# Where the weights' sums of a seven-product block are made, and 96 bytes less of padding

## Chip, cores, metric

One core of a Trainium2 chip runs the whole kernel as one program. The metric is the device time of one execution in microseconds (us). Of the kernel before, three executions were timed (median 883.89 us, 883.29 to 884.83), and one more was recorded by the profiler.

## What is computed

A linear attention feeds a two-layer feed-forward block, all in float32:

```python
q_s = softmax(q, axis=-1)            # 8 batches, 8 heads, 576 positions, 64 wide
k_s = softmax(k, axis=2)             # over the positions
kv  = einsum('bhsd,bhse->bhde', k_s, v)
x   = einsum('bhsd,bhde->bhse', q_s, kv)   # to 4608 tokens x 512
out = (maximum(x @ w_in, 0) ** 2) @ w_out  # 512 -> 2048 -> 512
```

## The kernel before

**Tiles.** The 4608 tokens are worked in nine tiles of 512: tile t (0 to 7) has the first 512 positions of batch t, and tile 8 the last 64 positions of all eight batches. The 2048 inner columns are 16 chunks f of 128. For each chunk TensorE (PE) makes `h` (128 x 512, line 100's helper, `first`) from w_in's chunk and x, VectorE (DVE) and ScalarE (ACT) square its positive part, and PE adds its product with w_out's chunk to four accumulators `acc` (`second`), two chunks behind `first`. Every float32 factor is split into a high and a low part (`gh`, `gl`, `xh`, `xl`, and two halves of each weight), and each product is three matmuls of 512 columns: high by high, high by low, low by high. So a chunk's `h` is 12 matmuls and its `acc` another 12. `h` has two PSUM buffers: `h` of chunk f + 2 can begin only when DVE has written `gl` of chunk f, which reads `h` last.

**Beside that.** While tile t runs, DVE, ACT, GpSimd (POOL) and the DMA queue of SyncE (SP) prepare the attention of batch t + 1, one pair of heads after another. Near a tile's beginning (f = 1) and at f = 5, 9 and 13, DVE runs a chain of small operations on `bst` (the row statistics of q, 128 x 18), a product with q and a transpose; it begins when a swap of `bst` between partitions by four small DMAs has landed. POOL takes the column maximum of k over the partitions (`kmx`). Each engine runs its instructions in order; the order of tile 0 is made by a planner, everything behind it runs in the order of the code.

**The joint block.** Tiles 7 and 8 are worked together, two chunks at a time (eight pairs n), by seven products in place of eight half-size ones: with a11 to a22 the quarters of the pair's weights (rows are the pair's two chunks, columns the two halves of the inner dimension) and b11 to b22 those of the tokens, the products need the weights' sums s1 = a21 + a22, s2 = s1 - a11, s3 = a11 - a21, s4 = a12 - s2, and the tokens' differences t1 to t4 (`ahead`, in tile 6). A product is six matmuls of 512 columns, in the order a11, a12, s2, s1, s3, a22, s4. Two PSUM buffers A and Bk take them; DVE and ACT combine them to c11, c22, c21 and c12. Of these, c11 and c21 (tile 7) are split to gh and gl at once (`use_g`), and c22 and c12 (tile 8) are stored to memory (`keep_g`, `g_last`). Between the products, units of three matmuls of the pair before (`unit`) are worked off.

**The sums before.** In tiles 1 to 4, at f = 1 and 9, `full_sums` and `add_sums` make one pair's sums on POOL (two additions of 512 columns, four operations of 256). At f = 3 and 11 `begin_sums` stores the pair's a11, a12 and a22 to the memory tensor `w_sums` of that pair, at f = 4 and 12 the sums are split (ACT casts, DVE subtracts), and at f = 7 and 15 `keep_sums` stores them. The joint block loads all seven pieces of a pair one or two pairs ahead (`load_weights`), into slabs 0, 1, 14 and 15 for even pairs and into other buffers (`ring`) for odd ones. A slab is one chunk of w_in, high and low part. Slabs 4 to 13 hold the tokens' pieces there; t3's low part lies in slab 13.

**Memory.** In SBUF the pools stand one behind the other: const, att, cvt, ffn, tiny, and then `boot`, which is closed after the start and replaced by `late`. Weights are held as 16 words of two chunks each (word 0 has chunks 0 and 1 of w_in, word u from 1 to 14 has chunk u + 1 of w_in and u - 1 of w_out, word 15 the last two of w_out); words 0 to 11 lie in const and 12 to 15 in `late`. `tiny`, the small pool, begins with a pad of 92 numbers (line 398), `late` with one of 16.

Of the kernel before, what the change touches and what calls it, by code (L numbers as in the profile page):

```python
# [10 lines left out]
F32 = mybir.dt.float32  # L11
F32R = mybir.dt.float32r
# [4 lines left out]
ALU = mybir.AluOpType  # L17
# [319 lines left out]
def attention_ffn(  # L337
# [29 lines left out]
    P = 128  # L367
# [27 lines left out]

    const, att, cvt = pool("const", 1), pool("att", 1), pool("cvt", 2)
    ffn, tiny = pool("ffn", 2), pool("tiny", 1)
    tiny.pool.tile([P, 92], F32, tag="pad2", name="pad2")
    boot_ctx = ExitStack()
    boot = Pool(boot_ctx.enter_context(tc.tile_pool(name="boot", bufs=3)), 3, True)  # L400
    ps_o, ps_h, ps_a = (pool(n, d, space=PSUM) for n, d in (("ps_o", 1), ("ps_h", 2), ("ps_a", 1)))
# [637 lines left out]
    def second(f, parts, acc, c, begin=0, end=NF - 1):  # L1039
        gh, gl = parts  # L1040
        cs = slice(c * P, (c + 1) * P)
        with plan.together(True):
            for n, (a, w) in enumerate(((gh, wo_h), (gh, wo_l), (gl, wo_h))):
# [2 lines left out]
                    start=(f == begin and n == 0), stop=(f == end and n == 2),  # L1046
                )

    def begin_sums(j):

        one, two = slabs[2 * j], slabs[2 * j + 1]
        for q, (slab, cols) in enumerate(
            ((one, slice(0, HM)), (one, slice(HM, M)), (two, slice(HM, M)))
        ):
            Y.dma_start(
                out=w_sums[j][:, 4 * q + 2:4 * q + 4, :], in_=slab[:, :, cols].bitcast(F32)
            )

    def full_sums(j):

        one, two = slabs[2 * j], slabs[2 * j + 1]
        full = cvt.tile([P, 2, M], F32, tag="w", name=f"full_{j}")
        for i, slab in enumerate((one, two)):
            G.tensor_tensor(out=full[:, i, :], in0=slab[:, 0, :], in1=slab[:, 1, :], op=ALU.add)
        made["full", j] = full

    def add_sums(j):

        full = made.pop(("full", j))
        (a11, a12), (a21, a22) = ((full[:, i, 0:HM], full[:, i, HM:M]) for i in range(2))  # L1070
        sums = cvt.tile([P, 4, HM], F32, tag="w", name=f"sums_{j}")
        s1, s2, s3, s4 = (sums[:, n, :] for n in range(4))
        G.tensor_tensor(out=s1, in0=a21, in1=a22, op=ALU.add)
        G.tensor_tensor(out=s2, in0=s1, in1=a11, op=ALU.subtract)
        G.tensor_tensor(out=s3, in0=a11, in1=a21, op=ALU.subtract)
        G.tensor_tensor(out=s4, in0=a12, in1=s2, op=ALU.subtract)
        made["sums", j] = sums.rearrange("p n c -> p (n c)")

    def split_sums(j):

        sums = made.pop(("sums", j))
        hi = cvt.tile([P, 2, M], F32R, tag="w", name=f"sums_h_{j}").rearrange("p t n -> p (t n)")
        lo = sums.bitcast(F32R)
        for i in range(2):
            S.copy(out=hi[:, i * M:(i + 1) * M], in_=sums[:, i * M:(i + 1) * M])
        made["split", j] = hi, lo, sums

    def rest_sums(j):

        hi, lo, sums = made["split", j]  # L1090
        for i in range(2):
            at = slice(i * M, (i + 1) * M)
            V.tensor_tensor(out=lo[:, at], in0=sums[:, at], in1=hi[:, at], op=ALU.subtract)
# [29 lines left out]
        return w  # L1123

    SOURCE = {"s1": 0, "a11": 2, "s2": 4, "a12": 6, "s3": 8, "a22": 10, "s4": 12}

    def load_weights(n, w, *names):

        for name in names if w else ():
            at = SOURCE[name]  # L1130
            Y.dma_start(out=w[name].bitcast(F32), in_=w_sums[n][:, at:at + 2, :])

    def pieces(name, t):

# [241 lines left out]
    def sums_step(t, f):  # L1376

        j, i = divmod(f, NF // 2)
        j += 2 * (t - 1)
        if t < 1 or j >= NF // 2:  # L1380
            return
        if i == 1:
            full_sums(j)
            add_sums(j)
        elif i == 3:
            begin_sums(j)
        elif i == 4:
            split_sums(j)
            rest_sums(j)
        elif i == 7:  # L1390
            keep_sums(j)

    x_of, w_of = {}, {}
# [1 line left out]
    def take(name, eng, out, in0, in1):  # L1395

        for i in range(2):
            eng.tensor_tensor(out=out[i], in0=in0[i], in1=in1[i], op=ALU.subtract)
        made[name] = out
# [7 lines left out]
    def ahead(f, x):  # L1407

        k = range(2)
        if f == 4:  # L1410
            made["b11"] = [x[:, i, :] for i in k]
            made["b21"] = [x[:, 2 + i, :] for i in k]
            made["b12"], made["b22"] = (
                [slabs[X_RAW + j].bitcast(F32)[:, i, :] for i in k] for j in range(2)
            )
            for i in k:
                to = slabs[X_RAW + i].bitcast(F32)[:, :, 0:(B - 1) * TL]
                Y.dma_start(out=to, in_=x_tail[:, 2 * i:2 * i + 2, 0:(B - 1) * TL])
            w_of[0] = weights(0)
            load_weights(0, w_of[0], "a11", "s1", "a12", "s2")  # L1420
        elif f == 6:
            split_x_of("b11")
        elif f == 9:
            temps = [att.tile([P, M], F32, tag=tag, name=f"sum_{tag}") for tag in ("k", "q")]
            take("t1", G, temps, made["b12"], made["b11"])
        elif f == 11:
            split_x_of("t1")
        elif f == 12:
            split_x_of("b21")
            take("t2", V, made["t1"], made["b22"], made["t1"])  # L1430
        elif f == 13:
            split_x_of("t2")
            take("t3", V, made["b11"], made["t2"], made["b11"])
        elif f == 14:
            split_x_of("t3")
            take("t4", V, made["b21"], made["b21"], made["t2"])
        elif f == 15:
            load_weights(0, w_of[0], "s3", "a22", "s4")
            split_x_of("b22")
# [63 lines left out]
    def unit(count):  # L1503

        for t, f, parts_u, acc_u, c, begin, end in units[:count]:
            second(f, parts_u, acc_u, c, begin=begin, end=end)
            if f == end:
                store(t, acc_u, c)
        del units[:count]
# [6 lines left out]
    def use_g(f, c, tags, eng):  # L1516

        V.scalar_tensor_tensor(out=c, in0=c, scalar=0.0, in1=c, op0=ALU.max, op1=ALU.mult)
        split_last(f, c, tags, eng, WT)
# [21 lines left out]
    for n in range(PAIRS):  # L1541
        one, two = 2 * n, 2 * n + 1
        units_at = (0, 1, 1, 1, 1) if n else (3, 0, 1, 0, 0)
        w = w_of.pop(n)
        A, Bk = (ps_h.tile([P, M], F32, tag="h", name=f"h_{WT}_{f}") for f in (two, one))
        u1, u2, u3 = (
            ffn.tile([P, M], F32, tag=tag, name=f"u_{tag}_{n}", bufs=1) for tag in ("xh2", "xl2", "xh3")
        )
        c11, c21 = (ffn.tile([P, M], F32, tag="r", name=f"c_{WT}_{f}") for f in (one, two))
        c22, c12 = (att.tile([P, M], F32, tag="ek", name=f"c_{B}_{f}", bufs=2) for f in (two, one))  # L1550
        if n == 0:
            split_x_of("t4")
        unit(units_at[0])

        product(A, w["a11"], x_of["b11"], True)
        S.copy(out=u1, in_=A)
        unit(units_at[1])
        product(Bk, w["a12"], x_of["b21"], True)
        V.tensor_tensor(out=c11, in0=Bk, in1=u1, op=ALU.add)
        use_g(one, c11, one_tags, G)  # L1560
        if n == PAIRS - 1:
            load_g(0)
            load_g(1)
        unit(units_at[2])
        product(A, w["s2"], x_of["t2"], False)
        S.copy(out=u2, in_=A)
        if n == 0:
            w_of[1] = weights(1)
            load_weights(1, w_of[1], "a11", "s1", "a12", "s2", "s3", "a22", "s4")
        elif n + 2 < PAIRS:  # L1570
            w_of[n + 2] = weights(n + 2)
        unit(units_at[3])
        product(Bk, w["s1"], x_of["t1"], True)
        if n == 0:
            w_of[2] = weights(2)
        load_weights(n + 2, w_of.get(n + 2), "a12", "s2", "a11", "s1")
        unit(units_at[4])
        product(A, w["s3"], x_of["t3"], False)
        S.copy(out=u3, in_=A)
        V.tensor_tensor(out=c22, in0=Bk, in1=u3, op=ALU.add)  # L1580
        keep_g(two, c22)
        if n == PAIRS - 1:
            load_g(2)
        unit(2)
        product(A, w["a22"], x_of["t4"], False)
        load_weights(n + 2, w_of.get(n + 2), "s3", "a22")
        S.copy(out=c21, in_=A)
        unit(1)
        product(Bk, w["s4"], x_of["b22"], False)
        load_weights(n + 2, w_of.get(n + 2), "s4")  # L1590
        V.tensor_tensor(out=c12, in0=Bk, in1=u2, op=ALU.add)
        tags = ((att, "v", 2), (att, "k" if n % 2 else "q", None))
        use_g(two, c21, tags, V)
        keep_g(one, c12)
        if n == PAIRS - 1:
            load_g(3)
        unit(1)
        if acc is None:
            acc = begin_acc(WT)
        units += [(WT, f, parts[WT, f], acc, c, 0, NF - 1) for f in (one, two) for c in range(C)]  # L1600
# [54 lines left out]
```

## Time and profile before

| | |
|---|---|
| median of three timed executions | 883.89 us |
| the profiled execution | 886.97 us |
| its span, first to last instruction | 885.2 us |
| instructions | 12559 |
| data moved | 95.52 MB |
| q1, the queue of SP and ACT: share of 16 DMA engines | 36.2% |

The profile names an instruction by its line, engine, operation and tiles, written left of the arrow and read right of it; nearly all instructions are recorded through one helper at line 100, so one goes by the tiles' names. A timeline row has start, duration, engine and shape, and in brackets how long the engine stood idle before and what ended that. A row of the chain that ended last has start, duration and what ran. In group rows the numbers behind the bar are busy time in us and the mean of one in ns. PE's rows of duration 0.39 overlap, since matmuls are pipelined; the pace is the distance between starts. Places in the span: tile 0 begins about 61 us in, tile 2 at 234, tile 5 at 524, and the joint block at 711.

### The profile page before, as it was taken

To read this page: it belongs to the slowest core of one execution; us is meant where nothing else is said; L and a number is where in the kernel's file an instruction comes from. 1 tells how busy PE (TensorE), PEld (TensorE's weight loads), DVE (VectorE), ACT (ScalarE), POOL (GpSimd) and SP (SyncE) were. 2 spreads that over 40 slices of the span, in tenths; PEclk is the share of its full clock that TensorE was granted. 3 is DMA by queue.
4 is the path that set the end of the run, shared out by engine and by line. 5 is a ranking of instruction groups with operands and counts; after the bars stand their busy time and mean duration, and the time that the engine had idled before them with its cause. 6 is when DMAs were issued, how large, how long until landed. Compare 5 with 4: busy or idle time off the path is not lost.

```text
span 885.2 us, 12559 instructions
## 1 busy us (share of the span) xinstructions
PE 862.2 (97%) x4408; PEld 705.4 (80%) x4408; DVE 571.2 (65%) x1092; ACT 377.5 (43%) x719; POOL 181.2 (20%) x211
## 2 busy tenths in 40 slices
PE   7899999999999999999999999999999999999997
PEld 6678877788878887888878888888887888888786
DVE  6988978766676767666766766676677653433421
ACT  5888854333533343334433353334343432222221
POOL 6789982020020202020202000000001001010000
PEclk9999999999999999999999999999999999999999
DMA  9992121413433243323232242122341175542432
GB/s 283 387 325 58 36 50 66 110 51 84 130 86 86 70 131 85 87 74 92 73 87 74 74 139 51 27 50 63 87 120 34 36 238 156 170 149 81 153 115 48
DMA packets 164367, 95.52 MB, mean 108 GB/s; under 512 B 113104, under 2 KB 146384, under 8 KB 164304
## 3 DMA queue, kind: packets, MB, share of 16 engines
q1 hardware_dynamic: 162592, 93.41, 36.2%
q10 hardware_dynamic: 1712, 1.31, 0.5%
q8 instruction: 35, 0.57, 0.3%
q14 instruction: 28, 0.23, 0.1%
HBM read 64.88 MB, written 29.23 MB: 106 GB/s over the span
## 4 chain that ended last, share of the span: by engine, by line
PE 81%; DVE 7%; DMA 4%; SPq 3%; ACT 2%; issue 1%; DVEq 0%; ACTq 0%
PE acc L100 40%; PE h L100 28%; PE h L1157 9%; SPq L100 3%; DVE bst L100 3%; PE x L100 3%; PE kv L100 2%; DMA raw<-in_moe_w_out_dram 2%; DMA k<-in_k_dram 1%; DVE q L100 1%; DMA bst<-bst 1%; DVE km L100 1%; DVE gl L100 1%; DVE h L100 1%; DVE qT L100 0%
## 5 line engine op out<-in xcount | busy, mean ns | idle before, releaser
L100 PE MATMUL acc<-w,gh 128*128 128x512 f32 x1152 | 357.9, 392 | 0.0
L100 PE MATMUL h<-xh,w 128*128 128x512 f32 x896 | 298.7, 396 | 8.3 <-DVE v L100 6.0
L100 PEld LDWEIGHTS acc<-w,gh 128*128 128x128 f32 x1152 | 214.8, 188 | 46.1 <-ACT gh L100 0.4
L100 PE MATMUL acc<-w,gl 128*128 128x512 f32 x576 | 225.5, 392 | 0.0
L100 PEld LDWEIGHTS h<-xh,w 128*128 128x128 f32 x896 | 169.1, 189 | 47.3 <-DVE v L100 7.7
L100 PE MATMUL h<-xl,w 128*128 128x512 f32 x448 | 176.0, 393 | 0.0
L100 PEld LDWEIGHTS acc<-w,gl 128*128 128x128 f32 x576 | 108.2, 188 | 24.2 <-DVE gl L100 0.4
L100 DVE TENSOR_TENSOR gl<-h,gh 128x512 fp32r<-128x512 f32 x112 | 77.2, 690 | 68.6 <-ACT gh L100 58.8
L100 ACT ACTIVATE gh<-r 128x512 fp32r<-128x512 f32 x112 | 70.7, 631 | 91.0 <-PE acc L100 89.3
L100 POOL PARTITION_ALL_REDUCE kmx<-km x24 | 17.1, 713 | 418.9 <-DVE km L100 418.9
L100 DVE SCALAR_TENSOR_TENSOR h<-h,r 128x512 f32<-128x512 f32 x112 | 77.2, 690 | 39.6 <-ACT r L100 39.0
L100 PEld LDWEIGHTS h<-xl,w 128*128 128x128 f32 x448 | 84.5, 189 | 17.1
L100 ACT ACTIVATE r<-h 128x512 f32<-128x512 f32 x112 | 66.4, 593 | 61.9 <-PE h L100 61.6
L100 ACT ACTIVATE q<-q 128x576 f32<-128x576 f32 (+1 forms) x32 | 21.5, 673 | 72.0 <-DVE q L100 70.8
L100 DVE TENSOR_REDUCE bst<-q 128x18 f32<-128x576 f32 x48 | 35.9, 748 | 13.9 <-ACT q L100 13.5
L100 DVE TENSOR_TENSOR bst<-bst 128x18 f32<-128x18 f32 (+1 forms) x96 | 29.0, 302 | 23.7 <-DMA bst<-bst 14.8
L100 POOL TENSOR_TENSOR w<-w,raw 128x512 int32<-128x512 int32 x32 | 42.1, 1323 | 7.7 <-DVE w L100 3.7
L100 DVE TENSOR_TENSOR c<-h,u_xh 128x512 f32<-128x512 f32 x16 | 11.1, 692 | 49.4 <-ACT u_xh L100 41.5
L100 POOL TENSOR_TENSOR w<-w,w 128x512 fp32r<-128x512 f32 x32 | 41.1, 1299 | 4.3 <-ACT w L100 4.2
L100 DVE TENSOR_TENSOR q<-q,bst 128x576 f32<-128x576 f32 x48 | 40.3, 839 | 1.7
L100 POOL TENSOR_TENSOR gl<-c,gh 128x512 fp32r<-128x512 f32 x8 | 10.3, 1292 | 131.0 <-ACT gh L100 131.0
L100 ACT ACTIVATE raw<-raw 128x1024 f32<-128x1024 f32 (+1 forms) x32 | 36.3, 1150 | 1.4 <-DMA raw<-in_moe_w_in_dram 1.1
(151 smaller groups left out, 960.5 us busy)
## 6 DMA issues: line engine op xcount, KB each, us to landing
k<-in_k_dram SPq DMA_DIRECT2D x32, 256.0 KB, 2.9
raw<-in_moe_w_in_dram SPq DMA_DIRECT2D x16, 512.0 KB, 8.6
raw<-in_moe_w_out_dram SPq DMA_DIRECT2D x16, 512.0 KB, 9.1
out_dram<-o SPq DMA_DIRECT2D x32, 256.0 KB, 2.4
v<-in_v_dram SPq DMA_DIRECT2D x56, 128.0 KB, 2.9
w<-w_sums SPq DMA_DIRECT2D x28, 256.0 KB, 3.3
q<-in_q_dram SPq DMA_DIRECT2D x96, 72.0 KB, 2.3
w_sums<-w SPq DMA_DIRECT2D x24, 256.0 KB, 3.1
```

Source lines behind the costliest of these rows:

```text
L100: getattr(self.eng, op)(*map(real, args), **{k: real(a) for k, a in kwargs.items()})
L1157: nc.tensor.matmul(out=out.real(), lhsT=a[:, k * P:(k + 1) * P].real(), rhs=m[k].real(), start=(begin and k == 0 and i == 0), stop=(k == 1 ...
```

## The change

Four things are edited.

- **Six pairs' sums move into the joint block.** `OWN = 2`: for pairs 2 to 7 the sums are made while the pair before is worked, by a new function `own_sums` in six steps placed between the products, and never stored. For these, `begin_sums` stores a21 as a fourth piece, `load_weights` skips s1 to s4, and `own_sums` loads a21 at the pair's beginning. Each step is two operations of 256 columns on DVE (eight additions and subtractions that also add the halves of a quarter, then four that take the high part off, behind four casts on ACT).
- **Two pairs' sums stay in the tiles**, pair 0 in tile 2 and pair 1 in tile 3, on DVE in place of POOL and spread over f = 4, 8, 10 and 12, with the split at f = 12 and 13 and the store at f = 14.
- **POOL's other subtractions on this path move to DVE**: t1 in tile 6 (from f = 9 to f = 10) and gl of c11 in every pair.
- **The pad** of the small pool has 68 numbers in place of 92: all of that pool behind the pad, and `boot` and `late`, move down by 96 bytes.

```diff
-    tiny.pool.tile([P, 92], F32, tag="pad2", name="pad2")
+    tiny.pool.tile([P, 68], F32, tag="pad2", name="pad2")
...
+    OWN = 2
...
+        for at, slab, cols in (
+            (2, one, slice(0, HM)), (6, one, slice(HM, M)), (10, two, slice(HM, M)),
+            (14, two, slice(0, HM)),
+        )[:3 if j < OWN else 4]:
+            Y.dma_start(out=w_sums[j][:, at:at + 2, :], in_=slab[:, :, cols].bitcast(F32))
...
-            G.tensor_tensor(out=full[:, i, :], in0=slab[:, 0, :], in1=slab[:, 1, :], op=ALU.add)
...
+        V.tensor_tensor(
+            out=made["full", j][:, i, :], in0=slab[:, 0, :], in1=slab[:, 1, :], op=ALU.add
+        )
...
+            if n >= OWN and name in SUMS:
+                continue
...
+    def own_sums(n, w, step):
...
+        if step == 0:
+            made["own"] = [
+                cvt.tile([P, 4, HM], F32, tag="w", name=f"own_{kind}_{n}") for kind in ("a", "s")
+            ]
+            Y.dma_start(out=made["own"][0][:, 0:2, :], in_=w_sums[n][:, 14:16, :])
+            return
...
+        for out, (in0, in1), op in (
+            ((a21, (a21, a22), ALU.add), (a22, two("a22"), ALU.add)),
+            ((a11, two("a11"), ALU.add), (a12, two("a12"), ALU.add)),
+            ((s1, (a21, a22), ALU.add), (s2, (s1, a11), ALU.subtract)),
+            ((s3, (a11, a21), ALU.subtract), (s4, (a12, s2), ALU.subtract)),
+            (), (),
+        )[step - 1]:
+            V.tensor_tensor(out=out, in0=in0, in1=in1, op=op)
+        if step > 4:
+            for i in (0, 1) if step == 5 else (2, 3):
+                hi, lo = two(SUMS[i])
+                S.copy(out=hi, in_=s[:, i, :])
+                V.tensor_tensor(out=lo, in0=s[:, i, :], in1=hi, op=ALU.subtract)
...
-            take("t1", G, temps, made["b12"], made["b11"])
+            take("t1", V, temps, made["b12"], made["b11"])
...
-        use_g(one, c11, one_tags, G)
+        use_g(one, c11, one_tags, V)
+        own_sums(n + 1, w_next, 1)
```

The instruction order of POOL behind tile 0: first the one before, from the third maximum of tile 1's batch to the second of tile 2's (`full` and `sums` are the sums, the bare ISA rows reload POOL's function library).

```order
L100 ISA kmx_3_2325<-km_3_2322 128x128
L100 ISA kmx_0_2618<-km_0_2615 128x128
L100 ISA
L100 TENSOR_TENSOR full_2672<-w_797 128x512
L100 TENSOR_TENSOR full_2672<-w_854 128x512
L100 TENSOR_TENSOR sums_2675<-full_2672 128x256
L100 TENSOR_TENSOR sums_2675<-sums_2675,full_2672 128x256
L100 TENSOR_TENSOR sums_2675<-full_2672 128x256
L100 TENSOR_TENSOR sums_2675<-full_2672,sums_2675 128x256
L100 ISA
L100 ISA kmx_1_2781<-km_1_2778 128x128
```

The same stretch of POOL now:

```order
L100 ISA kmx_2_2127<-km_2_2124 128x128
L100 ISA kmx_3_2302<-km_3_2299 128x128
L100 ISA kmx_0_2588<-km_0_2585 128x128
L100 ISA kmx_1_2744<-km_1_2741 128x128
L100 ISA kmx_2_2978<-km_2_2975 128x128
```

From tile 1 on POOL has nothing left but the maxima, and no reloads between them.

DVE in pair 2 of the joint block before, from c11 to the relu of c12 (`c_4` is first c11 and then c12, `c_5` first c22 and then c21):

```order
L100 TENSOR_TENSOR c_4_7175<-h_4_7168,u_xh_2_7163 128x512
L100 SCALAR_TENSOR_TENSOR c_4_7175<-c_4_7175 128x512
L100 TENSOR_TENSOR c_5_7217<-h_4_7168,u_xh_2_7215 128x512
L100 SCALAR_TENSOR_TENSOR c_5_7217<-c_5_7217 128x512
L100 TENSOR_TENSOR c_4_7247<-h_4_7168,u_xl_2_7191 128x512
L100 SCALAR_TENSOR_TENSOR c_5_7235<-c_5_7235 128x512
L100 TENSOR_TENSOR gl_5_7252<-c_5_7235,gh_5_7250 128x512
L100 SCALAR_TENSOR_TENSOR c_4_7247<-c_4_7247 128x512
```

And now, from the relu of c11 on (`own_a` holds a21, a22, a11, a12, `own_s` s1 to s4, `ring` the next pair's weights):

```order
L100 SCALAR_TENSOR_TENSOR c_4_7102<-c_4_7102 128x512
L100 TENSOR_TENSOR gl_4_7107<-c_4_7102,gh_4_7105 128x512
L100 TENSOR_TENSOR own_a_7081<-own_a_7081 128x256
L100 TENSOR_TENSOR own_a_7081<-ring_a_3_7048 128x256
L100 TENSOR_TENSOR own_a_7081<-ring_7012 128x256 x2
L100 TENSOR_TENSOR own_s_7135<-own_a_7081 128x256
L100 TENSOR_TENSOR own_s_7135<-own_s_7135,own_a_7081 128x256
L100 TENSOR_TENSOR c_5_7149<-h_4_7095,u_xh_2_7147 128x512
L100 SCALAR_TENSOR_TENSOR c_5_7149<-c_5_7149 128x512
L100 TENSOR_TENSOR own_s_7135<-own_a_7081 128x256
L100 TENSOR_TENSOR own_s_7135<-own_a_7081,own_s_7135 128x256
L100 TENSOR_TENSOR ring_7012<-own_s_7135,ring_7012 128x256 x2
```

Six sums and gl stand between c11 and c22; s3, s4 and the first two low parts stand between c22 and c12, the other two low parts behind c12's relu.

SP at the same place before, from the store of c12 of pair 1 to that of pair 2:

```order
L100 DMA g_last<-c_2_7144 128x512
L100 DMA w_382<-w_sums_111 128x512 x4
L100 DMA g_last<-c_5_7217 128x512
L100 DMA w_1487<-w_sums_111 128x512 x2
L100 DMA w_1576<-w_sums_111 128x512
L100 DMA g_last<-c_4_7247 128x512
```

And now:

```order
L100 DMA g_last<-c_2_7065 128x512
L100 DMA own_a_7081<-w_sums_110 128x512
L100 DMA w_382<-w_sums_111 128x512 x2
L100 DMA g_last<-c_5_7149 128x512
L100 DMA w_1487<-w_sums_111 128x512
L100 DMA g_last<-c_4_7183 128x512
```

Three loads of a pair's weights are left of seven, and the load of a21 stands right behind the store of the pair before.

More of the change, by code (lines that the diff above doesn't have):

```diff
@@ L1047, in second @@
                 )
+    OWN = 2
     def begin_sums(j):
         one, two = slabs[2 * j], slabs[2 * j + 1]
[L1052 to L1063, printed above, removed]
-            G.tensor_tensor(out=full[:, i, :], in0=slab[:, 0, :], in1=slab[:, 1, :], op=ALU.add)
-        made["full", j] = full
@@ L1067, in add_sums @@
-    def add_sums(j):
-        full = made.pop(("full", j))
-        (a11, a12), (a21, a22) = ((full[:, i, 0:HM], full[:, i, HM:M]) for i in range(2))
[L1071 to L1077, printed above, removed]
+        for at, slab, cols in (
[3 more added lines that the diff above has]
+            Y.dma_start(out=w_sums[j][:, at:at + 2, :], in_=slab[:, :, cols].bitcast(F32))
@@ new lines, in full_sums, with add_sums @@
+    def full_sums(j, i):
+        if i == 0:
+            made["full", j] = cvt.tile([P, 2, M], F32, tag="w", name=f"full_{j}")
+        slab = slabs[2 * j + i]
+        V.tensor_tensor(
+            out=made["full", j][:, i, :], in0=slab[:, 0, :], in1=slab[:, 1, :], op=ALU.add
+        )
+    def add_sums(j, n):
+        full = made["full", j]
+        (a11, a12), (a21, a22) = ((full[:, i, 0:HM], full[:, i, HM:M]) for i in range(2))
+        if n == 0:
+            made["sums", j] = cvt.tile([P, 4, HM], F32, tag="w", name=f"sums_{j}")
+        s1, s2, s3, s4 = (made["sums", j][:, i, :] for i in range(4))
+        out, in0, in1, op = (
+            (s1, a21, a22, ALU.add), (s2, s1, a11, ALU.subtract),
+            (s3, a11, a21, ALU.subtract), (s4, a12, s2, ALU.subtract),
+        )[n]
+        V.tensor_tensor(out=out, in0=in0, in1=in1, op=op)
@@ L1079, in split_sums @@
     def split_sums(j):
-        sums = made.pop(("sums", j))
+        sums = made.pop(("sums", j)).rearrange("p n c -> p (n c)")
         hi = cvt.tile([P, 2, M], F32R, tag="w", name=f"sums_h_{j}").rearrange("p t n -> p (t n)")
-        lo = sums.bitcast(F32R)
         for i in range(2):
             S.copy(out=hi[:, i * M:(i + 1) * M], in_=sums[:, i * M:(i + 1) * M])
-        made["split", j] = hi, lo, sums
+        made["split", j] = hi, sums.bitcast(F32R), sums
     def rest_sums(j):
@@ L1125, in attention_ffn, with two @@
     SOURCE = {"s1": 0, "a11": 2, "s2": 4, "a12": 6, "s3": 8, "a22": 10, "s4": 12}
+    SUMS = "s1", "s2", "s3", "s4"
     def load_weights(n, w, *names):
         for name in names if w else ():
+            if n >= OWN and name in SUMS:
+                continue
             at = SOURCE[name]
             Y.dma_start(out=w[name].bitcast(F32), in_=w_sums[n][:, at:at + 2, :])
+    def own_sums(n, w, step):
+        if n < OWN or n >= PAIRS:
+            return
[4 more added lines that the diff above has]
+            Y.dma_start(out=made["own"][0][:, 0:2, :], in_=w_sums[n][:, 14:16, :])
+            return
+        a, s = made["own"]
+        a21, a22, a11, a12 = (a[:, i, :] for i in range(4))
+        s1, s2, s3, s4 = (s[:, i, :] for i in range(4))
+        def two(name):
+            return w[name][:, 0, :], w[name][:, 1, :]
+        for out, (in0, in1), op in (
[5 more added lines that the diff above has]
+        )[step - 1]:
+            V.tensor_tensor(out=out, in0=in0, in1=in1, op=op)
+        if step > 4:
[3 more added lines that the diff above has]
+                V.tensor_tensor(out=lo, in0=s[:, i, :], in1=hi, op=ALU.subtract)
     def pieces(name, t):
@@ L1379, in sums_step @@
         j += 2 * (t - 1)
-        if t < 1 or j >= NF // 2:
+        if t >= 1 and j < NF // 2 and i == 3:
+            begin_sums(j)
+        j = t - 2
+        if j not in range(OWN):
             return
[L1382 to L1387, printed above, removed]
+        if f == 4:
+            full_sums(j, 0)
+        elif f == 8:
+            full_sums(j, 1)
+        elif f == 10:
+            for n in range(3):
+                add_sums(j, n)
+        elif f == 12:
+            add_sums(j, 3)
             split_sums(j)
+        elif f == 13:
             rest_sums(j)
-        elif i == 7:
+        elif f == 14:
             keep_sums(j)
@@ L1422, in ahead @@
             split_x_of("b11")
-        elif f == 9:
+        elif f == 10:
             temps = [att.tile([P, M], F32, tag=tag, name=f"sum_{tag}") for tag in ("k", "q")]
-            take("t1", G, temps, made["b12"], made["b11"])
+            take("t1", V, temps, made["b12"], made["b11"])
         elif f == 11:
@@ L1544, in attention_ffn @@
         w = w_of.pop(n)
+        w_next = w_of.get(n + 1)
+        own_sums(n + 1, w_next, 0)
         A, Bk = (ps_h.tile([P, M], F32, tag="h", name=f"h_{WT}_{f}") for f in (two, one))
@@ L1566, in attention_ffn @@
         S.copy(out=u2, in_=A)
+        own_sums(n + 1, w_next, 2)
         if n == 0:
@@ L1576, in attention_ffn @@
         load_weights(n + 2, w_of.get(n + 2), "a12", "s2", "a11", "s1")
+        own_sums(n + 1, w_next, 3)
         unit(units_at[4])
@@ L1581, in attention_ffn @@
         keep_g(two, c22)
+        own_sums(n + 1, w_next, 4)
         if n == PAIRS - 1:
@@ L1587, in attention_ffn @@
         S.copy(out=c21, in_=A)
+        own_sums(n + 1, w_next, 5)
         unit(1)
@@ L1594, in attention_ffn @@
         keep_g(one, c12)
+        own_sums(n + 1, w_next, 6)
         if n == PAIRS - 1:
```

## Prediction, made before the change was run

> **What bounds the kernel now.** I read the page first (engine totals), then PE's waits, then the chain that ended last, then engine timelines at the places where PE stood still, and last the chain's durations by place, to see whether PE runs at one pace. The page's first part:
>
> ```profile
> PE 862.2 (97%) x4408; PEld 705.4 (80%) x4408; DVE 571.2 (65%) x1092; ACT 377.5 (43%) x719; POOL 181.2 (20%) x211
> ```
>
> PE is busy for 97% of the span, so only what gives PE fewer gaps or a quicker pace can shorten the run. The change leaves PE's instructions as they are. PE's largest wait, by its own view of waits (total us, times, longest):
>
> ```profile
> PE h L100 <- DVE v L100: 6.0, 4, 1.8
> ```
>
> Four waits in 885 us, all at the head of a tile (tiles 1 to 4). This is the one of tile 2, on PE; the bracket is the idle time and its releaser:
>
> ```profile
> 250.24 0.39 PE L100 MATMUL acc<-w,gl 128*128 128x512 f32 x1
> 252.18 0.50 PE L100 MATMUL h<-xh,w 128*128 128x512 f32 x1 [1.54 <-DVE v L100]
> ```
>
> The memset of v named there is a neighbour; what PE needs is the gl subtraction just before it on DVE, which frees the PSUM bank for the next h. DVE (first fence) and POOL (second) ahead of that moment:
>
> ```profile
> 243.70 1.92 DVE L100 TENSOR_TENSOR bst<-bst 128x18 f32<-128x18 f32 x2 [1.75 <-DMA bst<-bst]
> 246.47 0.76 DVE L100 SCALAR_TENSOR_TENSOR bst<-bst 128x18 f32<-128x18 f32 x1
> 247.96 1.25 DVE L100 TENSOR_TENSOR q<-q,bst 128x576 f32<-128x576 f32 x1
> 251.44 0.68 DVE L100 TENSOR_TENSOR gl<-h,gh 128x512 fp32r<-128x512 f32 x1
> ```
>
> ```profile
> 243.03 2.53 POOL L100 TENSOR_TENSOR full<-w 128x512 f32<-128x512 f32 x2 [7.33 <-DMA bst<-bst]
> 245.64 0.74 POOL L100 TENSOR_TENSOR sums<-full 128x256 f32<-128x256 f32 x1
> 246.46 0.74 POOL L100 TENSOR_TENSOR sums<-sums,full 128x256 f32<-128x256 f32 x1
> ```
>
> And the same DVE instructions at the head of tile 5, where POOL makes no sums:
>
> ```profile
> 534.61 0.41 DVE L100 TENSOR_TENSOR bst<-bst 128x18 f32<-128x18 f32 x2 [2.63 <-DMA bst<-bst]
> 535.55 0.18 DVE L100 SCALAR_TENSOR_TENSOR bst<-bst 128x18 f32<-128x18 f32 x1
> 536.27 0.76 DVE L100 TENSOR_TENSOR q<-q,bst 128x576 f32<-128x576 f32 x1
> 539.26 0.68 DVE L100 TENSOR_TENSOR gl<-h,gh 128x512 fp32r<-128x512 f32 x1
> ```
>
> Two small bst operations take 1.92 us instead of 0.41, and end when POOL's `full` ends (243.03 + 2.53 = 245.56, against 245.62). From the first bst operation to the end of gl it is 8.42 us with POOL's sums (252.12 - 243.70) and 5.33 us without (539.94 - 534.61). At heads 5 and 6 PE has no such wait. So POOL's sums hold VectorE up, and VectorE holds PE up.
>
> **What goes at the heads of tiles 1 to 4.** POOL's sums go from all tiles. In tile 2, gl would end at 243.70 + 5.33 = 249.0; PE is ready for h at 250.24 + 0.23 = 250.5. The wait goes and 1.4 us are to spare; next late would be the bst swap's DMA. The worth: 6.0 us of idle. The step from 250.24 to 252.18 is 1.94, of which 1.54 is idle and 0.23 a matmul's own pace: 0.17 more per stop, 0.7 in all. PE also restarts slowly; the chain's lines give the first twelve matmuls of h after a stop (tiles 1, 2 and 4), and of tile 5 without one:
>
> ```profile
> 156.02 3.02 PE h L100 x12
> 252.18 3.06 PE h L100 x12
> 444.45 4.61 PE h L100 x12
> 540.66 2.72 PE h L100 x12
> ```
>
> That is 0.3 us more each, 1.2 for four (4.61 holds the clock's part, below). Together 6.0 + 0.7 + 1.2 = 7.9 us.
>
> The 4.61 of tile 4 has another cause besides (the window's columns: length, busy time by engine, granted clock, DMA):
>
> ```profile
> 444.40:448.40 4.00, 3.95 (x10) 3.13 (x11) 3.80 (x7) 0.28 (x1) 0.73 (x1) 0.57 0.85 218
> ```
>
> The granted clock was 0.57 here, behind the stop of tile 4. It cost 4.61 - 3.02 = 1.6 us of this execution. Whether the timed runs have it the trace doesn't say; the profiled execution took 886.97 us, 3.1 more than the median of 883.89, so I take the dip as its own. The Trainium skill (TensorE: Matmul & The Clock Gate, Part 1) has the clock fall to half after an idle window of about 3.4 us; here the longest wait was 1.8 us (no run here shows a longer one ahead of a dip), so by that rule the stop was not its cause, it could come again, and the next profiled execution would gain 1.6 us less.
>
> **Tile 6's first difference t1 moves from POOL to DVE.** PE (first fence) waits once more there, and DVE and POOL show why:
>
> ```profile
> 682.63 0.37 PE L100 MATMUL x<-qh,kvh 128*128 128x288 f32 x1 [0.92 <-ACT kvh L100]
> ```
>
> ```profile
> 676.70 1.15 DVE L100 TENSOR_TENSOR bst<-bst 128x18 f32<-128x18 f32 x1
> ```
>
> ```profile
> 676.53 1.28 POOL L100 TENSOR_TENSOR sum_k<-w,x 128x512 f32<-128x512 f32 x1 [7.26 <-ACT ek L100]
> ```
>
> The bst operation ends with POOL's (677.85 and 677.81). It is 1.0 us longer than it would be alone, on the chain to kvh; so this wait of 0.9 goes. On DVE the two differences cost 2 x 0.69 = 1.4 us, but behind kvl; next late there is gl of f = 11, whose bank PE wants back only after the products of h for f = 12 and of acc for f = 10, 2 x 2.72 us. Worth 0.9 us.
>
> **The pad.** In the built program the tiles of words 12 to 15 (pool `late`) begin at byte 195,936 of a partition, 96 past a multiple of 128; all other 128x512 operands of PE begin on a multiple of 128. 96 bytes less puts `late` on 195,840, a multiple too. Does PE care? Words 12 to 15 hold w_in's chunks 13 to 15 and w_out's 11 to 15. The chain in tile 2 (acc of f = 10, then h of 13 and acc of 11), and two products of the joint block (weights in the `att` ring, then in slab 15, a late one):
>
> ```profile
> 302.11 2.72 PE acc L100 x12
> 304.83 2.81 PE h L100 x12
> 307.63 2.80 PE acc L100 x12
> ...
> 756.75 1.36 PE h L1157 x6
> ...
> 752.62 1.40 PE h L1157 x6
> ```
>
> PE slows exactly where the late tiles begin: 0.08 in 12 or 0.04 in 6, 6.7 ns a matmul (1.36 / 6 = 0.2267 us, 1.40 / 6 = 0.2333). That is 3%, or 15 of a matmul's 512 columns: close to the 16 numbers of one more 64-byte piece, which is what a start off a grid of 64 would add to every read. The count: in tiles 0 to 6, 3 x 12 matmuls of h and 5 x 12 of acc each, 672; the two last tiles' acc, 120; in the joint block, s3, a22 and s4 of the four even pairs, 72, and two of six with t3's low part in the odd pairs, 8. 872 x 6.7 ns = 5.8 us. Bounds: 0 if the place and not the start is slow; 6.5 if the followers that share the slow pace (not counted) gain too. I take 5.8: the count fits the alignment. Against it speak tile 0's x products, whose boot tiles begin 32 past a multiple of 128 (first and last of six, then the same six in tile 1's end, aligned):
>
> ```profile
> 28.57 0.30 PE L100 MATMUL x<-qh,kvh 128*128 128x288 f32 x1
> 29.23 0.30 PE L100 MATMUL x<-ql,kvh 128*128 128x288 f32 x1
> ...
> 224.70 0.29 PE L100 MATMUL x<-qh,kvh 128*128 128x288 f32 x1
> 225.37 0.29 PE L100 MATMUL x<-ql,kvh 128*128 128x288 f32 x1
> ```
>
> 0.66 and 0.67 us: no 6.7 ns each here. These boot tiles share the addresses of word 15, so they speak against a slow place as much as against a slow start; hence a rival, not an answer. The Trainium skill (SBUF — State Buffer, Specifications) gives lines of 16 bytes; 195,936 is a multiple of 16, so by it the pad gives nothing, and the sum is the first rival's.
>
> **The joint block's new work.** Six pairs get 8 additions and 4 subtractions of 256 columns on DVE, 4 casts on ACT, and POOL's gl moves to DVE. DVE's price, and the moves:
>
> ```profile
> L100 DVE TENSOR_TENSOR xl<-x,xh 128x288 fp32r<-128x288 f32 x4 | 1.8, 443 | 0.3 <-ACT xh L100 0.3
> w<-w_sums SPq DMA_DIRECT2D x28, 256.0 KB, 3.3
> raw<-in_moe_w_out_dram SPq DMA_DIRECT2D x16, 512.0 KB, 9.1
> ```
>
> 443 ns for 288 columns, so about 0.42 for 256: 12 x 0.42 + 0.69 = 5.7 us of DVE in a pair of 15.1. It hides in DVE's gaps; pair 2 (DVE, then ACT's gh and SP's store of c12):
>
> ```profile
> 743.13 0.69 DVE L100 TENSOR_TENSOR c<-h,u_xh 128x512 f32<-128x512 f32 x1 [0.91 <-PE h L1157]
> 750.14 0.69 DVE L100 TENSOR_TENSOR c<-h,u_xh 128x512 f32<-128x512 f32 x1 [5.58 <-ACT u_xh L100]
> ```
>
> ```profile
> 744.64 0.62 ACT L100 CAST gh<-c 128x512 fp32r<-128x512 f32 x1 [3.00 <-DVE c L100]
> ```
>
> ```profile
> 742.26 0.32 SPq L100 DMA_DIRECT2D g_last<-c  x1
> ```
>
> gl can start at 745.3 and ends at 746.0. a21, the last of the sums' inputs, comes by a new load behind that store on SP: issued at 742.6, landing 3.3 later, 745.9. Six sums then end at 748.5, before c22 at 750.1. c22 must be done before s4's product (752.62), so 3.4 us are to spare. The other six fall behind c22 and c21, where s1 to s4 are used only in the next pair; 4 casts of some 0.4 us fit ACT's gaps of 3.0. Reloads fall from seven a pair to four. Cost 0, bounds 0 and the slow rival.
>
> **Tiles 2 and 3** get six sums and the two rest subtractions on DVE (up to 1.3 us at f = 10). Cover: at f = 9 POOL stretches DVE today as at the head, and PE does not wait:
>
> ```profile
> 292.35 1.24 DVE L100 TENSOR_TENSOR q<-q,bst 128x576 f32<-128x576 f32 x1
> ```
>
> That goes, so the sums take its room. SP has one store more at f = 3 and 11 of tiles 2 to 4, and two less at f = 7 and 15. Cost 0.
>
> **Sum.** 7.9 + 0.9 + 5.8 = 14.6 us, and the dip's 1.6 in the profiled execution: 886.97 - 16.2 = 870.8 there, and 883.89 - 14.6 = 869.3 for the median.
>
> **Rivals.** 1. Late tiles stay slow, being slow by place: 883.89 - 8.8 = 875.1. For it the boot tiles and the 16-byte lines; against it that the loss has the size of one piece. 18%.
> 2. The heads stay late in part: in tile 5 the swap's DMA let DVE start at 534.61 and gl ended 0.5 us before PE came. If the swaps come 2 us later than now, half of 7.9 stays: 873.3. 6%.
> 3. Slower: the sums' wait for a21 holds c22, since DVE runs in order, and c22 holds s4's product. It costs from a landing of 3.3 + 3.4 = 6.7 us on, and eats the gain of 14.6 at 2.4 us a pair, 9.1 us, which only the raw words show, in the loaded start. At 10 us: 6 x 3.3 = 19.8 more, 889.1. 3%.
> 4. Nothing measurable, because both gains are absent from unprofiled runs: 883.9. 3%.
>
> **Numbers.** The forecast has 70%. The range reaches down by the dip (1.6), the followers (0.7) and the spread of runs (0.5) to 866.5, and up to rival 1 with 0.9 and 1.0 of spread, 877.0. About 0.2% (1.8 us) can be told from no change: faster 0.94, same 0.03, slower 0.03.
>
> **What would show it.** Right: no wait of h on DVE at heads 1 to 4, bst pairs at 0.41, chain pieces of 2.72 at f = 13 to 15, DVE's idle before c22 down by some 3 us. Wrong: 2.80 there (rival 1), brackets of a us or more on h (2), or PE waiting on DVE in the joint block (3).

## The result, and the profile after

The changed kernel takes 877.28 us against 883.83: a ratio of 0.9922 (95% interval 0.9909 to 0.9934), 6.6 us gained (5.8 to 8.0). The forecast was 869.3, with a range that ended at 877.0. The profiled execution took 876.96 us, where the prediction had 870.8; its span is 875.2. One of the four executions of a later kernel (tile 6's differences back on GpSimd, below) took 1735.78 us, twice the others, and is left out of its median and ratio.

To find where the rest is, I cut both spans at the same four matmuls (PE's order is the same in both): tile 0's head, the joint block's first and last, the end. Before (first fence) and after (second); the second column is the length, the third PE's busy time (then PEld, DVE, ACT and POOL, the granted clock, the DMA engines' share and GB/s):

```profile
0.00:61.01 61.01, 50.15 (x343) 41.46 (x344) 50.54 (x106) 45.77 (x85) 45.24 (x68) 1.00 1.00 326
61.01:711.18 650.17, 642.87 (x3332) 526.32 (x3331) 460.95 (x899) 290.46 (x564) 125.61 (x136) 1.00 0.29 79
711.18:831.13 119.95, 119.95 (x524) 98.18 (x523) 44.51 (x67) 29.06 (x52) 10.34 (x8) 1.00 0.48 156
831.13:885.20 54.07, 49.27 (x213) 39.46 (x211) 15.20 (x23) 12.20 (x21) 0.00 (x0) 1.00 0.35 107
```

```profile
0.00:65.48 65.48, 49.75 (x343) 40.93 (x344) 50.48 (x106) 45.87 (x85) 44.73 (x68) 1.00 1.02 336
65.48:702.76 637.28, 636.09 (x3332) 525.10 (x3331) 440.79 (x901) 285.18 (x552) 79.63 (x86) 1.00 0.27 70
702.76:821.30 118.54, 118.54 (x524) 98.16 (x523) 76.07 (x147) 36.10 (x76) 0.00 (x0) 1.00 0.37 118
821.30:875.20 53.90, 48.79 (x213) 39.45 (x211) 15.20 (x23) 12.27 (x21) 0.00 (x0) 0.98 0.36 108
```

From tile 0's head on, the change gains 12.9 + 1.4 + 0.2 = 14.5 us. But the start, where by the prediction nothing changed, is 4.5 us longer. PE's waits name the place; this is the top of that view, after:

```profile
PE idle L1383 <- POOL ident masks.py:199: 9.8, 1, 9.8
PE h L100 <- DVE gl L100: 2.3, 2, 2.0
```

The four waits of h on DVE at the heads of tiles 1 to 4 (6.0 us) are gone; the 2.3 stood in this view before as well. At the top stands a wait for `ident`, the identity matrix that PE needs for its first transposes, 9.8 us where it was 1.6. (`idle` is the name of a tile: PE begins with ten filler transposes into it, which nobody reads and which need `ident` too.) POOL at the start, before (first fence) and after (second):

```profile
0.72 0.20 POOL masks.py:197 MEMSET ident<- 128x128 f32 x1 [0.29 <-POOLq L1635]
1.22 0.29 POOL masks.py:199 TENSOR_SCALAR_AFFINE_SELECT ident<-ident 128x128 f32<-128x128 f32 x1 [0.29 <-POOL ident masks.py:197]
```

```profile
0.72 0.20 POOL masks.py:197 MEMSET ident<- 128x128 f32 x1 [0.29 <-POOLq L1686]
9.45 0.28 POOL masks.py:199 TENSOR_SCALAR_AFFINE_SELECT ident<-ident 128x128 f32<-128x128 f32 x1 [8.53 <-issue]
```

The same two instructions, in the same order: but after the change POOL stands still for 8.5 us ahead of the second, and no semaphore is waited for ("issue").

The rest came out much as foretold. The head of tile 2 on DVE, after; the bst pair takes 0.41 again, and PE's chain across that point has no stop:

```profile
245.29 0.41 DVE L100 TENSOR_TENSOR bst<-bst 128x18 f32<-128x18 f32 x2 [1.69 <-DMA bst<-bst]
246.96 0.76 DVE L100 TENSOR_TENSOR q<-q,bst 128x576 f32<-128x576 f32 x1
249.95 0.68 DVE L100 TENSOR_TENSOR gl<-h,gh 128x512 fp32r<-128x512 f32 x1
```

```profile
246.85 2.72 PE h L100 x12
249.57 2.72 PE acc L100 x12
252.29 2.72 PE h L100 x12
...
304.57 2.72 PE h L100 x12
307.29 2.72 PE acc L100 x12
```

The last two pieces use the late tiles (h of f = 13, acc of f = 11); they were 2.81 and 2.80. In the joint block PE is busy for the whole of its 118.54 us. DVE has the new sums in its gaps there; pair 2's, with c22 at 741.04:

```profile
737.41 0.42 DVE L100 TENSOR_TENSOR own_a<-own_a 128x256 f32<-128x256 f32 x1 [0.30 <-DMA own_a<-w_sums]
...
741.04 0.69 DVE L100 TENSOR_TENSOR c<-h,u_xh 128x512 f32<-128x512 f32 x1 [1.28 <-ACT u_xh L100]
```

DVE waits for a21's load three times in the block (1.78, 0.30 and 0.28 us), and this holds PE up nowhere; DVE's idle time before c22 fell from 5.58 to 1.28.

### The profile page after: what moved, and what is told of

Its sections match the earlier page's. It is cut to its first block, busy times and chain, and to the rows that moved or that the text cites. A ratio compares the mean times of both kernels' runs of the same rounds, so it can differ in the third digit from the quotient of the medians.

```text
span 875.2 us, 12474 instructions
## 1 busy us (share of the span) xinstructions
PE 853.2 (97%) x4408; PEld 703.6 (80%) x4408; DVE 582.5 (67%) x1174; ACT 379.4 (43%) x731; POOL 124.4 (14%) x153
## 4 chain that ended last, share of the span: by engine, by line
PE 89%; DVE 4%; DMA 3%; SPq 3%; ACT 1%; issue 0%; DVEq 0%; ACTq 0%
PE acc L100 43%; PE h L100 32%; PE h L1193 9%; SPq L100 3%; PE x L100 3%; PE kv L100 2%; DMA raw<-in_moe_w_out_dram 1%; DMA q<-in_q_dram 1%; DVE bst L100 1%; DVE km L100 1%; DVE h L100 1%; DMA kt<-in_k_dram 0%; DVE gl L100 0%; DMA bst<-bst 0%; DVE q L100 0%
## 5 line engine op out<-in xcount | busy, mean ns | idle before, releaser
L100 PE MATMUL acc<-w,gh 128*128 128x512 f32 x1152 | 355.8, 390 | 0.0
L100 PE MATMUL h<-xh,w 128*128 128x512 f32 x896 | 295.8, 392 | 2.3 <-DVE gl L100 2.3
L100 PEld LDWEIGHTS acc<-w,gh 128*128 128x128 f32 x1152 | 214.7, 188 | 43.9 <-ACT gh L100 0.4
L100 PE MATMUL acc<-w,gl 128*128 128x512 f32 x576 | 224.2, 389 | 0.0
L100 PEld LDWEIGHTS h<-xh,w 128*128 128x128 f32 x896 | 168.2, 188 | 38.4 <-DVE gl L100 2.4
L100 PE MATMUL h<-xl,w 128*128 128x512 f32 x448 | 174.5, 389 | 0.0
L100 PEld LDWEIGHTS acc<-w,gl 128*128 128x128 f32 x576 | 108.1, 188 | 23.1 <-DVE gl L100 0.4
L100 DVE TENSOR_TENSOR gl<-h,gh 128x512 fp32r<-128x512 f32 x112 | 77.1, 689 | 71.2 <-ACT gh L100 61.7
L100 ACT ACTIVATE gh<-r 128x512 fp32r<-128x512 f32 x112 | 70.7, 631 | 92.7 <-PE acc L100 90.3
L100 DVE SCALAR_TENSOR_TENSOR h<-h,r 128x512 f32<-128x512 f32 x112 | 77.2, 690 | 45.2 <-ACT r L100 44.6
L100 PEld LDWEIGHTS h<-xl,w 128*128 128x128 f32 x448 | 84.1, 188 | 16.3
L100 ACT ACTIVATE r<-h 128x512 f32<-128x512 f32 x112 | 66.4, 593 | 65.2 <-PE h L100 64.9
L100 POOL PARTITION_ALL_REDUCE kmx<-km x24 | 16.9, 703 | 509.2 <-DVE km L100 509.2
L100 ACT ACTIVATE q<-q 128x576 f32<-128x576 f32 (+1 forms) x32 | 21.6, 674 | 70.3 <-DVE q L100 62.3
L100 DVE TENSOR_REDUCE bst<-q 128x18 f32<-128x576 f32 x48 | 35.9, 748 | 13.9 <-ACT q L100 13.5
L100 POOL TENSOR_TENSOR w<-w,raw 128x512 int32<-128x512 int32 x32 | 42.1, 1325 | 6.5 <-DVE w L100 3.7
L100 POOL TENSOR_TENSOR w<-w,w 128x512 fp32r<-128x512 f32 x32 | 41.1, 1299 | 4.7 <-ACT w L100 4.5
L100 DVE TENSOR_TENSOR q<-q,bst 128x576 f32<-128x576 f32 x48 | 36.4, 758 | 1.7
L100 ACT ACTIVATE raw<-raw 128x1024 f32<-128x1024 f32 (+1 forms) x32 | 36.3, 1148 | 0.1
L1193 PE MATMUL h<-w,w 128*128 128x512 f32 x144 | 36.0, 389 | 0.0
L100 DVE TENSOR_TENSOR bst<-bst 128x18 f32<-128x18 f32 (+1 forms) x96 | 17.8, 186 | 23.6 <-DMA bst<-bst 14.8
L100 DVE TENSOR_TENSOR ql<-qT,qh 128x576 fp32r<-128x576 f32 (+1 forms) x32 | 23.6, 739 | 14.1 <-ACT qh L100 12.9
```

What stands on the lines that cost most here:

```text
L100: getattr(self.eng, op)(*map(real, args), **{k: real(a) for k, a in kwargs.items()})
L1193: nc.tensor.matmul(out=out.real(), lhsT=a[:, k * P:(k + 1) * P].real(), rhs=m[k].real(), start=(begin and k == 0 and i == 0), stop=(k == 1 ...
```

## The experiments

**The start.** What differs at POOL's end? In the kernel before, POOL's last partition reduction was followed by ten additions and subtractions (tile 6's two differences and eight low parts in the joint block). The change took all of them away. The row of the first of the ten in the prediction read `[7.26 <-ACT ek L100]`: POOL idle for 7.26 us between the last reduction and sum_k. The trace has an instruction MODIFY_POOL_CONFIG, twice in a row, wherever a reduction follows other arithmetic or the reverse: at 18 places behind the start in the kernel before, at one in the changed one. At nine of the 18 arithmetic follows a reduction, and starts 7.0 to 7.7 us behind the instruction; at six of these the profile names no wait:

```profile
POOL full L100 <- issue: 42.7, 6, 7.4
```

(At the other nine the reduction starts 6.2 to 8.9 us behind it, but always 0.1 us after VectorE has written its operand, so these lengths tell nothing of the exchange.) The instruction also stands ahead of `ident` in both kernels, at 1.12 us before (first fence) and 0.94 us after (second); the row has number, duration in ns, and first and last start:

```profile
masks.py:199 POOLq MODIFY_POOL_CONFIG  x2: 11/11/11, 1.1 to 1.1; - x2
```

```profile
masks.py:199 POOLq MODIFY_POOL_CONFIG  x2: 11/11/11, 0.9 to 1.0; - x2
```

Yet only in the changed kernel do 8.5 us follow it. Theory: POOL's code for the two kinds of work is exchanged, and what the program ends with is what its next execution finds. The Trainium skill (GPSIMD Engine Reference, Instruction dispatch) has GpSimd's code loaded at run time by that instruction, at about 6 us for the first call; the trace agrees in kind, with 7.0 to 7.7 behind a reduction.

Rival: the late start belongs to the program as built. The first kernel gives the kernel before the same end, and leaves the rest:

```
-            take("t1", G, temps, made["b12"], made["b11"])
+            take("t1", V, temps, made["b12"], made["b11"])
...
-        use_g(one, c11, one_tags, G)
+        use_g(one, c11, one_tags, V)
```

> The kernel before with GpSimd's ten last operations (tile 6's two differences and the joint block's eight low parts) on VectorE, so that GpSimd's last operation is a partition reduction. Theory of the reload: identity at about 9.5 us, 4.5 us lost by the first tile's head, 0.4 to 0.9 gained in tile 6: 883.8 + 4.5 - 0.6 = 887.7 us. Rival (something else of the change delays the start): 883.2.

Measured: ratio 1.0051 (1.0030 to 1.0072), 889.64 us against 885.11 on that chip; slower by 4.5 us where 3.9 was expected. POOL and PE at its start:

```profile
9.27 0.28 POOL masks.py:199 TENSOR_SCALAR_AFFINE_SELECT ident<-ident 128x128 f32<-128x128 f32 x1 [8.35 <-issue]
```

```profile
PE idle L1347 <- POOL ident masks.py:199: 9.6, 1, 9.6
```

No sums were moved and no pad cut here, and the loss is there. The opposite: the changed kernel, with one addition of one column at the end of the program.

```
     unit(len(units))
+    nc.gpsimd.tensor_tensor(
+        out=zeros[:, 0:1], in0=zeros[:, 1:2], in1=zeros[:, 2:3], op=ALU.add
+    )
```

> The changed kernel plus one GpSimd addition of one column at the very end of the program (its operands are ready from the start, so it runs as soon as GpSimd's queue is empty). Theory: the 4.5 us by which the changed kernel comes later to the first tile's head are a reload of GpSimd's code for the identity matrix, needed because the program now ends on a partition reduction and the next execution finds that code loaded. With an addition last, the identity's instruction starts at about 1.2 us instead of 9.45 and PE's first transpose at about 4.9 instead of 11.97; 877.3 - 4.5 = 872.8 us. Rival: the late start belongs to the program as built (its instruction fetch) or to this load; then the start stays at 9.45 and the time at 877.3.

Measured: ratio 0.9858 (0.9834 to 0.9882), 873.24 us. POOL at the start, and where the added operation lies:

```profile
1.21 0.29 POOL masks.py:199 TENSOR_SCALAR_AFFINE_SELECT ident<-ident 128x128 f32<-128x128 f32 x1 [0.29 <-POOL ident masks.py:197]
...
657.95 0.70 POOL L100 PARTITION_ALL_REDUCE kmx<-km  x1 [16.27 <-DVE km L100]
665.28 0.18 POOL L1672 TENSOR_TENSOR zeros<-zeros 128x1 f32<-128x1 f32 x1 [6.63 <-issue]
```

The exchange has moved from the start, where PE waits for it, to 658 to 665 us, where nobody does. The first instructions of the program, as the trace shows them, are the same as in the changed kernel; what differs ahead of the identity is what the execution before left behind. The rival falls. (What another program, run in between, would leave behind was not tried.) The two once more on one chip, and a third that undoes a single move (tile 6's two differences back on GpSimd, by the first line above with V and G exchanged):

> The changed kernel once more, on the same chip as the two below. GpSimd's reload at the start is there in every execution, so the ratio to before is 0.992 to 0.993 again (some 6.5 us), and the identity's instruction starts at about 9.4 us.

> The kernel of warm_end once more beside it: ratio to before 0.986 to 0.987, 4 to 6 us below the changed kernel on the same chip. Rival (the distance seen so far was one of chips): no difference to the changed kernel.

> The changed kernel with tile 6's two differences on GpSimd as before, and nothing else undone. They follow the last partition reduction, so the program ends with the other code loaded: identity at about 1.2 us without any instruction added, some 4.5 us less than the changed kernel; in tile 6 the wait for kvh of about 1.0 us is there again instead of the two of 0.65 and 0.42 us, so nothing is lost or gained there. Ratio to before some 0.987. Rival (either of the two moves alone makes the start late, since GpSimd's code is chosen by the program as a whole): identity at 9.4 us, 0.992.

Measured: 0.9910 (0.9889 to 0.9931) for the changed kernel, 0.9859 (0.9836 to 0.9881) with the addition, 0.9858 (0.9827 to 0.9890) with the differences back; medians 876.63, 872.21 and 872.46 us. In the third, POOL exchanges its code in tile 6, as it did before the change:

```profile
656.43 0.70 POOL L100 PARTITION_ALL_REDUCE kmx<-km  x1 [16.28 <-DVE km L100]
664.34 1.28 POOL L100 TENSOR_TENSOR sum_k<-w,x 128x512 f32<-128x512 f32 x1 [7.21 <-ACT ek L100]
```

So the move of gl alone costs nothing at the start; both moves together cost 4.4 us (876.63 - 872.21). That the other move alone costs nothing either follows from the theory, but was not run. PE's first transpose comes 7.0 us later (11.97 against 4.94), yet tile 0's head only 4.4: 65.6 us on average in the four traces with a late identity (64.8 to 66.1), 61.3 in the nine others (59.8 to 64.3), which wait for loads there instead (`kT` on `k`, 2.4 us in the kernel before). Part of the spread is the clock: five of these traces have a granted clock of 0.50 for 3.4 us or more ahead of tile 0's head. Without these five it is 65.2 us (two traces) against 60.5 (six), 4.6 us.

**The pad.** Alone, in the kernel before (92 to 68 in the pad's line), and taken back in the changed one (68 to 92):

> The kernel before with the pad 96 bytes shorter and nothing else. Theory (an operand that begins off a multiple of 128 bytes costs PE some 6.5 ns a matmul): chain pieces of 2.72 us at f = 13 to 15, 883.8 - 6.4 = 877.4 us. Rival (the late tiles are slow by their place): 2.80 there, 883.8.

> The changed kernel with the pad at its old size, so the moved sums alone. Theory: PE's chains at f = 13 to 15 are at 2.80 again and 6.4 us come back, while the heads stay free of waits and the late start stays: ratio to before 0.9922 + 6.4/883.8 = 0.9994, no change that can be told. Rival (pad without effect): 0.992.

Measured: pad alone 0.9919 (0.9894 to 0.9944), the sums alone 0.9975 (0.9958 to 0.9991). The second was expected at 0.9994, just outside the interval. From tile 0's head to PE's last matmul the traces have 817.0 us for the kernel before (a second trace, below), 810.8 with the pad alone, 810.2 with the sums alone, 804.2 with both: 6.2, 6.8 and 12.8 us gained. h of f = 13 and acc of f = 11 in tile 2, with the pad alone (first fence) and taken back (second):

```profile
306.79 2.72 PE h L100 x12
309.51 2.72 PE acc L100 x12
```

```profile
306.25 2.81 PE h L100 x12
309.06 2.80 PE acc L100 x12
```

Is it the start's place in 64 bytes, as the prediction's count had it? The late pool has a pad of its own (16 numbers); on top of the kernel with the added operation it becomes 24 or 32, which moves words 12 to 15 and nothing else:

> The kernel of warm_end with the late pool's own pad 32 bytes longer: words 12 to 15 begin 32 past a multiple of 128 (and of 64), nothing else moves. If a start off a grid of 64 bytes costs one more piece of 64, chain pieces at f = 13 to 15 are 2.80 and the span is 6.4 us longer (some 879); if only a start in a certain part of 128 bytes costs, they stay at 2.72 (some 872.5). The place theory has 2.72 as well, so 2.80 would be its end.

> The kernel of warm_end with the late pool's own pad 64 bytes longer: words 12 to 15 begin 64 past a multiple of 128. Grid of 64: 2.72, span some 872.5. Grid of 128: 2.80, some 879.

Measured: spans of 876.4 and 873.7, of one execution each; from tile 0's head to PE's last matmul, which leaves the start out, 809.6 and 808.4 us against 804.4 of the kernel with the added operation. h and acc of the late tiles in tile 2, at 32 past a multiple of 128 (first fence) and at 64 (second):

```profile
304.33 2.80 PE acc L100 x12
307.13 2.79 PE h L100 x12
```

```profile
299.67 2.80 PE h L100 x12
302.47 2.76 PE acc L100 x12
```

Slow at 64 too, against the grid of 64. Over the 848 matmuls that read a late tile and are followed at once by another, the mean from start to start is 227.3 ns at 0 past a multiple of 128 (the changed kernel), 231.4 at 64, 232.9 at 32 and 233.6 at 96 (the kernel before). At 64 it is the chains that move the late tile (acc, 230.5) that lose less than those that load it as weights (h, 233.1). The place theory (the late tiles are slow by where they lie) falls as well: a shift of 32 bytes switches the loss on.

**The heads.** Does a sum on GpSimd cost only where it meets the chain that PE waits for? The kernel before with its sums on GpSimd, behind another reduction (splits at i = 6, not shown):

```
-        if i == 1:
+        if i == 4:
             full_sums(j)
             add_sums(j)
```

> The kernel before with GpSimd's sums of tiles 1 to 4 issued at f = 4 and 12 instead of 1 and 9, behind the second and the fourth partition reduction instead of the first and the third; their splits at f = 6 and 14. All of them stay on GpSimd, with the same code swaps and the same store traffic. Theory (GpSimd's code arrives 7 us behind the reduction at the head of a tile, so that the sums meet VectorE's bst chain there, and only there PE is due): the four waits of h at the heads (5.7 us) go, 6.2 us gained, ratio 0.993. Rival (the sums cost PE wherever they meet VectorE): waits of the same size at f = 4 to 6 and 12 to 14, ratio 1.000.

Measured: 0.9984 (0.9966 to 1.0002); its trace gains 2.7 us from tile 0's head on (817.0 - 814.4). DVE where the sums are now, in tile 2, and PE behind it in the second half:

```profile
261.53 1.45 DVE L100 TENSOR_TENSOR bst<-bst 128x18 f32<-128x18 f32 x2
264.68 1.24 DVE L100 TENSOR_TENSOR q<-q,bst 128x576 f32<-128x576 f32 x1
...
318.97 0.37 PE L100 MATMUL x<-qh,kvh 128*128 128x288 f32 x1 [0.36 <-ACT kvh L100]
```

The four stops at the heads are gone, 7.0 us matmul by matmul. But at eight places, around the x products, PE falls 0.3 to 0.9 us behind, 4.3 us together. "There, and only there" was wrong: the collision costs PE 1.7 us at a head and some 0.5 at these places. That the sums leave GpSimd is what brings the whole.

**The dip.** A second trace of the kernel before:

> The kernel before once more, for a second trace. If the clock dip behind tile 4's head (1.75 us) belongs to the kernel, it is there again; if it was that execution's own, the span is some 883.5 and PE's excess at the head of tile 4 is some 1.8 us like that of the other heads. The four waits of h, 6.0 us together, are expected in both cases.

Measured: a span of 882.7. The granted clock is 1.00 in the 4 us behind the stop at tile 4's head (first fence; 0.57 in the first trace), and the four waits of h are there (second):

```profile
443.56:447.56 4.00, 3.95 (x17) 3.29 (x18) 3.80 (x7) 0.28 (x1) 0.73 (x1) 1.00 0.83 210
```

```profile
PE h L100 <- DVE v L100: 5.7, 4, 1.7
```

Such stretches come elsewhere in other traces, though. In all thirteen PE waits 2.0 us once, some 18 us ahead of tile 0's head, and in four of them the granted clock is 0.50 for 3.4 us behind that wait, as here in the kernel with the sums alone:

```profile
48.35:51.76 3.41, 3.41 (x10) 2.63 (x9) 3.31 (x7) 3.15 (x5) 3.02 (x3) 0.50 1.09 218
```

## Why the prediction was wrong

The direction was right, and so were the two largest terms, the heads and the pad, in size; the time was outside the range because one cost was never counted.

- **The step that failed** is "The joint block's new work", with "POOL's gl moves to DVE" and, ahead of it, tile 6's two differences: both were costed on the engine that receives them. What GpSimd is left with was not asked. Taking the last arithmetic from it put the exchange of its code at the next execution's start, on the one chain that PE waits for there: 4.4 us, shown by undoing it in two ways and by making it in the kernel before. Two rows in the prediction had the sign, idle times of 7.33 and 7.26 us on GpSimd, each between a reduction and the next arithmetic. The profile put the one down to a DMA and the other to ACT; each of these ended 0.1 us ahead, by chance or because GpSimd needed it too. The six of nearly the same length for which it names no wait stood in no row of the prediction.
- **The heads**, 7.9 us: right, measured 7.1 (tiles 1 to 4 with the sums alone: 1.7, 1.6, 1.7 and 2.0 less than in the second trace of before). The waits were 5.7 there, 6.0 in the trace that I used.
- **Tile 6's differences**, 0.9 us: wrong. With the sums alone the tile takes 91.07 us, before 90.92. The wait for kvh (0.9) goes, but the two differences now stand on DVE ahead of h and of the copies of x; ACT, which must copy the rest of x first, waits 1.82 us for DVE there (0.69 before) and casts qh behind it, and PE waits 0.51 and 0.26 for qh and ql instead. I had named gl of f = 11 as next late, and not x.
- **The pad**, 5.8 us: right in size and in that the start decides; measured 6.2, of which some 0.8 lie with the other 512-column matmuls (some 2,480 by 0.3 ns), as the bound of 6.5 had it. The reason given, one more piece of 64 bytes, fell.
- **The joint block**, cost 0: right, apart from what its move did to the start. With the sums alone it takes 119.95 us, as before; the 1.4 us gained there are the pad's.
- **The clock dip**, 1.6 us of that one execution: right for that place; the second trace is without it. The rule of the 3.4 us of idle time, which the prediction cites, does not account for such stretches here: PE's waits just ahead of them were 1.4 to 2.0 us, and most such waits have none behind them.
- The rivals: slow late tiles, late heads and a late a21 did not come. None dealt with the start, since tile 0's order does not change.

In sum: 7.1 at the heads, nothing in tile 6 and 6.2 from the pad, each measured singly; both together gain 12.8 from tile 0's head on, and less 4.4 at the start that is 8.4 us by the traces. The timed runs have 6.6 (5.8 to 8.0) in the first comparison and 7.9 (6.1 to 9.8) in the second; what is left between them is less than the spread of the start (59.8 to 64.3 us in kernels with an early identity).

## What to carry to other kernels

When work leaves an engine, look at what that engine does last and first as well: here the program's end set how its next execution started, and one added operation of 0.18 us at a place where nobody waits gave back 4.4 us; that kernel (873.2 us and 872.2 on two occasions) is faster than the changed one and the one before. An idle time that has nearly the same length wherever it stands (6.9 to 7.6 us on GpSimd, nine times between a reduction and the next arithmetic) is likely to have a cause of its own, even where the profile names a neighbour: look for the places where it names none. And where a loss follows an operand's tile, shift that tile alone: one run of a pad settled start against place.

## What the runs showed of the hardware

- From GpSimd's MODIFY_POOL_CONFIG to its next operation it took 7.0 to 7.7 us behind a reduction (nine places in one execution of the kernel before), and 7.8 to 8.5 us at the start of a program whose last GpSimd operation had been a reduction (four traces); 0.1 us where it had been arithmetic (nine traces).
- 512-column matmuls with an operand that starts 32, 64 or 96 bytes past a multiple of 128 took 3 to 6 ns longer from start to start than at a multiple of 128 (227.3), with the operand moving or loaded as weights. The x products of 288 columns, whose moving operands lay at 0, 32 and 64, took 132 to 134 ns in all cases. What makes the difference stays open.
- Two small VectorE operations on two SBUF operands took 1.45 to 1.92 us instead of 0.41 while GpSimd added. The Trainium skill (SBUF — State Buffer, Who interferes with whom) calls the shared port pair an exclusive lock; the trace agrees, since in the pair of 1.92 us each of the two ends within 0.1 us of one of GpSimd's two additions.
- The granted clock was 0.50 for 3.4 us or, once, 6.8 us, ahead of the span's end, in six of thirteen traces; second traces of two of these kernels (the one before, and the one with the added operation) have no such stretch.
